# Two loads requested last, products taken two groups sooner and one more tile transposed by DMA, in a fused attention and GLU kernel

## The chip, the core and the metric

The kernel runs on one core of a Trainium2 chip. The metric is the device time of one execution in microseconds. Each run is compared with runs of the kernel before on the same chip in the same rounds. A ratio is the mean time of one kernel's fast runs over the mean of the other's fast runs of the same rounds; it is therefore not quite the ratio of the medians quoted beside it.

## The reference, cut to what matters

x is (1, 2048, 512) in bf16. It is normalized once and feeds two branches.

```python
xn = layernorm(x)
# A: 32 heads of 16, each position attends to 8 positions, 2 apart, at and before it
q, k, v = split(xn @ wqkv)
s = softmax_over_8(q * k_shifted) * v_shifted, summed, @ wo
# B: gated MLP of width 1792
g = silu((gelu(xn @ w_gate) * (xn @ w_up)) @ w_down)
out = x + s * g
```

## The kernel before

The sequence is cut into four chunks of 512 columns, each of four tiles of 128. A chunk goes through glu (14 groups of gate and up), qkv of the next chunk, then down, the attention sums and the output. Tiles 4 to 7 are chunk 1; their transposed form, xnT of chunk 1, is built during chunk 0's glu stage. Work of one stage is hung into the stream of another by `at`, which names the place where it is put into each engine's order.

Names in the lines below: g_ps and u_ps are the gate and up products, ge, u and h what becomes of them, y_ps the down product; pk are the q-k products, L_ps the logits (their sums), E the exponentials, pv the products of E and v, den_ps and o_ps their sums, s_ps the output product; tr is a transpose on TensorE.

```python
    load_x(TPQ, TPQ)
    for i, (lo, hi) in enumerate(((0, DF // 2), (DF // 2, DF))):
        load_w(wg_sb, B_w_gate, lo, hi)
        load_w(wu_sb, B_w_up, lo, hi)
        load_x((2 + i) * TPQ, TPQ)          # x of chunks 2 and 3
    # ...
    def transpose(t, copy=None):            # by TensorE: 4 matmuls, one copy on ScalarE
        tr = mm.tile([P, NC * P], BF16, name="tr", tag="mm")
        to_psum(t, range(NC), tr[:])
        from_psum(t, range(NC), tr[:], copy)
    def transpose_by_dma(t, cs=range(NC)):  # by DMA: one request for each 128x128 block
        for c in cs:
            nc.sync.dma_start(out=xnT[j][:, c, i * P : (i + 1) * P],
                              in_=xns[t][:, c * P : (c + 1) * P], transpose=True)
    # ...
        if i < 2:
            at(("glu", 0, i), transpose, TPQ + i)              # tiles 4 and 5
    # ...
    at(("glu", 0, 9), logits, 0)
    for i in range(8):                      # products of E and v on VectorE
        at(("glu", 0, 11 + i) if i < 3 else ("qkv", 1, 0), av_product, 0, i // 2, i % 2)
    # ...
    at(("glu", 0, 0), transpose_by_dma, TPQ + 2, (0, 1))
    at(("glu", 0, 0), load_v, 0)            # v_arr, four requests, after vT is written
    at(("glu", 0, 0), transpose_by_dma, TPQ + 2, (2, 3))
    at(("glu", 0, 0), transpose_by_dma, TPQ + 3)
    at(("glu", 0, 0), load_late_weights)    # wd, wo
```

All DMA requests above leave from one queue, SyncE's, in program order. The built program gives them eight completion semaphores in turn, so a request also waits until the one eight places before it has landed. v takes a round trip: vst is stored to vT in memory and read back, shifted, as v_arr.

The softmax here doesn't subtract the row's maximum and nothing guards it: scores larger than these inputs give would overflow.

Of the kernel before, what the change touches and what calls it, by code (L numbers as in the profile page):

```python
# [28 lines left out]
def kernel(  # L29
# [15 lines left out]
    DF = B_w_gate.shape[1]  # L45
    NT, NC, NF, NJ = S // P, D // P, DF // P, S // TQ
    TPQ = TQ // P
# [39 lines left out]
    def load_x(t, n=1):  # L87
        nc.sync.dma_start(
            out=x_sb[:, t : t + n, :],
            in_=x2d[t * P : (t + n) * P, :].rearrange("(t p) d -> p t d", p=P),  # L90
        )

    def load_w(dst, src, lo, hi):
        nc.sync.dma_start(
            out=dst[:, :, lo:hi], in_=src.rearrange("(k p) n -> p k n", p=P)[:, :, lo:hi]
        )
# [11 lines left out]
    load_x(3)  # L108
    load_wqkv(3)
    load_x(TPQ, TPQ)  # L110
    for i, (lo, hi) in enumerate(((0, DF // 2), (DF // 2, DF))):
        load_w(wg_sb, B_w_gate, lo, hi)
        load_w(wu_sb, B_w_up, lo, hi)
        load_x((2 + i) * TPQ, TPQ)

    def load_late_weights():
        nc.sync.dma_start(out=wd_sb[:], in_=B_w_down.rearrange("(k p) n -> p k n", p=P))
# [155 lines left out]
    def copy_out(j, fo, ps, i0=0, n=TQ, m=1, copy=None):  # L273

        which, c = divmod(fo, NC)
        if which == 0:
            if "q" not in st[j]:
                st[j]["q"] = qp.tile([P, NC, TQ], BF16, name="q_sb")
            dst = st[j]["q"][:, c : c + m, i0 : i0 + n]
        elif which == 1:  # L280
            dst = k_sb[j][:, c : c + m, PAD + i0 : PAD + i0 + n]
        else:
            if c // 2 not in st[j]["vst"]:
                st[j]["vst"][c // 2] = vsp.tile([P, 2, TQ], BF16, name="vst")
            dst = st[j]["vst"][c // 2][:, c % 2 : c % 2 + m, i0 : i0 + n]
        if copy is None:
            nc.scalar.activation(out=dst, in_=ps, func=AF.Copy)  # L287
        else:
            copy(out=dst, in_=ps)
        if which == 2 and (c + m) % 2 == 0 and i0 + n == TQ:  # L290
            r, lo = slice((c // 2) * 2 * P, (c // 2 + 1) * 2 * P), PAD + j * TQ
            nc.sync.dma_start(
                out=vT[r, lo : lo + TQ].rearrange("(c p) n -> p c n", p=P),
                in_=st[j]["vst"][c // 2][:],
            )

    def qkv(j, fo):
        ps = mm.tile([P, 1, TQ], F32, name="qkv_ps", tag="mm")
        project(ps[:, 0, :], wqkv_sb, fo * P, j)
        copy_out(j, fo, ps[:])  # L300
# [128 lines left out]
    def divide(j):  # L429
        oT = st[j]["oT"] = op.tile([P, NC, TQ], BF16, name="oT")  # L430
        for g in range(0, NC, 2):
            nc.vector.tensor_tensor(  # L432
                out=oT[:, g : g + 2, :],
                in0=st[j]["o"][:, g : g + 2, :],
                in1=st[j]["rb"][:].unsqueeze(1).to_broadcast([P, 2, TQ]),
                op=ALU.mult,
            )

    def glu(j, fc):
        g_ps = mm.tile([P, TQ], F32, name="g_ps", tag="mm")  # L440
        project(g_ps[:], wg_sb, fc * P, j)
        u_ps = mm.tile([P, TQ], F32, name="u_ps", tag="mm")
        project(u_ps[:], wu_sb, fc * P, j)
        ge = sm.tile([P, TQ], BF16, name="ge")
        nc.scalar.activation(out=ge[:], in_=g_ps[:], func=AF.Gelu_apprx_tanh)  # L445
        u = sm.tile([P, TQ], BF16, name="u")
        nc.scalar.activation(out=u[:], in_=u_ps[:], func=AF.Copy)  # L447
        h = hp.tile([P, TQ], BF16, name="h")
        nc.vector.tensor_tensor(out=h[:], in0=ge[:], in1=u[:], op=ALU.mult)  # L449
        st[j][fc] = h  # L450

    def down(j, tt, cols):

        n = cols.stop - cols.start
        y = mm.tile([P, n], F32, name="y_ps", tag="mm")
        for fc in range(NF):
            nc.tensor.matmul(  # L457
                y[:],
                lhsT=st[j][fc][:, tt * P : (tt + 1) * P],
                rhs=wd_sb[:, fc, cols],  # L460
                start=(fc == 0),
                stop=(fc == NF - 1),
            )
        sl = slp.tile([P, n], BF16, name="sl")
        nc.scalar.activation(out=sl[:], in_=y[:], func=AF.Silu)  # L465
        return sl

    def finish(j, tt, cols, sl):

        t, n = j * TPQ + tt, cols.stop - cols.start  # L470
        s = mm.tile([P, n], F32, name="s_ps", tag="mm")
        for g in range(NC):
            nc.tensor.matmul(  # L473
                s[:],
                lhsT=st[j]["oT"][:, g, tt * P : (tt + 1) * P],
                rhs=wo_sb[:, g, cols],
                start=(g == 0),
                stop=(g == NC - 1),
            )
        m = sm2.tile([P, n], BF16, name="m")  # L480
        nc.vector.tensor_tensor(out=m[:], in0=s[:], in1=sl[:], op=ALU.mult)  # L481
        o_t = sm4.tile([P, n], BF16, name="o_t")
        nc.vector.tensor_tensor(out=o_t[:], in0=m[:], in1=x_sb[:, t, cols], op=ALU.add)
        nc.sync.dma_start(out=out2d[t * P : (t + 1) * P, cols], in_=o_t[:])
# [4 lines left out]
    def at(key, fn, *args):  # L489
        side.setdefault(key, []).append((fn, args))  # L490

    def run(stage, j, i):
        for fn, args in side.get((stage, j, i), ()):
            fn(*args)

    for i in range(TPQ):
        at(("down", 0, 1), moments, 2 * TPQ + i)
        if i < 2:
            at(("glu", 0, i), transpose, TPQ + i)
        at(("down", 0, 2), normalize, 2 * TPQ + i)  # L500
        at(("glu", 1, 0) if i else ("down", 0, 3), transpose_by_dma, 2 * TPQ + i)
        at(("glu", 1, 10 + i), moments, 3 * TPQ + i)
        at(("qkv", 2, i), normalize, 3 * TPQ + i)
        at(("glu", 2, 0) if i else ("down", 1, 3), transpose_by_dma, 3 * TPQ + i)
# [2 lines left out]
        at(("glu", 0, w), qk_products, 0, [w], 0, NC)  # L507
    at(("glu", 0, 9), logits, 0)
    for i in range(8):
        at(("glu", 0, 11 + i) if i < 3 else ("qkv", 1, 0), av_product, 0, i // 2, i % 2)  # L510

    def sums(j):

        if j + 1 < NJ:
            nc.scalar.preload_act_table(AF.Exp)
        denominators(j)
        av_sums(j)
        if j + 1 < NJ:
            logits(j + 1)
        reciprocals(j)  # L520
        store_reciprocals(j)
        spread_reciprocals(j)
        if j + 1 < NJ:
            load_v(j + 1)
# [80 lines left out]
    for n, fo in enumerate((0, 2, 4, 6, 8, 10)):  # L605
# [4 lines left out]
            for i in range(2):  # L610
                project(ps[:, i, i0 : i0 + w], wqkv_sb, (fo + i) * P, 0, HQ + i0, w)
        copy_out(0, fo, ps[:], HQ, HQ, 2)
    at(("glu", 0, 0), transpose_by_dma, TPQ + 2, (0, 1))
    at(("glu", 0, 0), load_v, 0)
    at(("glu", 0, 0), transpose_by_dma, TPQ + 2, (2, 3))
    at(("glu", 0, 0), transpose_by_dma, TPQ + 3)
    at(("glu", 0, 0), load_late_weights)
    for j in range(NJ):
        for fc in range(NF):
            run("glu", j, fc)  # L620
            glu(j, fc)
        if j + 1 < NJ:

            for i, fo in enumerate((0, 1, 4, 5, 2, 3, 6, 7, 8, 9, 10, 11)):
                run("qkv", j + 1, i)
                qkv(j + 1, fo)
            full = slice(0, D)
            sl = []
            for tt in range(TPQ):
                run("down", j, tt)  # L630
                sl.append(down(j, tt, full))
                if tt == 0:
                    sums(j)
            divide(j)
            for tt in range(TPQ):
                finish(j, tt, full, sl[tt])
        else:
            full, half = slice(0, D), (slice(0, D // 2), slice(D // 2, D))
            sl = [down(j, tt, full) for tt in range(TPQ - 1)]
            divide(j)  # L640
            finish(j, 0, full, sl[0])
            finish(j, 1, full, sl[1])
            sl3 = down(j, 3, half[0])
            finish(j, 2, full, sl[2])
            finish(j, 3, half[0], sl3)
            sl3 = down(j, 3, half[1])
            finish(j, 3, half[1], sl3)
# [28 lines left out]
```

## Time and profile before

| | before |
|---|---|
| median time of the first three runs | 227.88 us (227.87 to 228.2) |
| span of the profiled run | 226.7 us |
| TensorE, VectorE, ScalarE busy | 98%, 67%, 58% |
| granted TensorE clock | 1.000 |
| transposes of chunk 1 by TensorE, by DMA | tiles 4 and 5, tiles 6 and 7 |

Read the engine shares first: when one engine is busy in 98% of the span, idle time elsewhere costs nothing, and any change must be judged by what it takes from that engine's stream or by the holes that it makes in it. The prediction shows the lines.

### The profile page before, as it was taken

The numbers are of one execution on the slowest core, as the hardware profiler recorded it, in microseconds if no ns is written. First come the engines' busy times: TensorE is split into PE (matmuls) and PEld (weight loads), VectorE is DVE, ScalarE is ACT, GpSimd is POOL, SyncE is SP. The second block draws the span as 40 slices with busy tenths as digits, with TensorE's granted clock in tenths as the row PEclk, the third lists the DMA queues.
The fourth block names the chain that finished last, engine by engine and source line by source line (L and its number), as shares of the span: only waits on it lengthen the run. The fifth ranks groups of instructions, "written<-read, shape, count | busy, mean of one in ns | idle before, by whom it ended". The sixth has DMA issues, their size and how long they took to land.

```text
span 226.7 us, 3637 instructions
## 1 busy us (share of the span) xinstructions
PE 222.4 (98%) x1342; PEld 107.9 (48%) x1342; DVE 152.2 (67%) x281; ACT 132.3 (58%) x209; POOL 21.4 (9%) x67
## 2 busy tenths in 40 slices
PE   8999999999999999999999999999999999999993
PEld 4995444444444444444444444444444444444453
DVE  5588961999995489969803859925934448971434
ACT  4388679767631767676752466676763356756210
POOL 1025961000040000320000000000000000000000
PEclk9999999999999999999999999999999999999999
DMA  6999399942049911100219941100218940001011
GB/s 191 361 397 385 102 211 162 309 121 95 6 99 198 196 48 30 21 1 0 93 34 205 191 112 23 26 6 0 92 25 167 198 113 0 0 3 30 1 39 54
DMA packets 30130, 24.64 MB, mean 109 GB/s; under 512 B 10784, under 2 KB 29600, under 8 KB 30112
## 3 DMA queue, kind: packets, MB, share of 16 engines
q1 hardware_dynamic: 30112, 24.41, 45.1%
q8 instruction: 10, 0.16, 0.3%
q14 instruction: 8, 0.07, 0.1%
HBM read 18.74 MB, written 4.34 MB: 102 GB/s over the span
## 4 chain that ended last, share of the span: by engine, by line
PE 98%; DVE 0%; issue 0%; DVEq 0%
PE y_ps L457 21%; PE g_ps L263 21%; PE u_ps L263 21%; PE qkv_ps L263 16%; PE s_ps L473 6%; PE L_ps L352 3%; PE o_ps L420 3%; PE qk_ps L551 2%; PE v_ps L551 1%; PE warm_ps L245 1%; PE qk_ps L542 1%; PE den_ps L372 0%; PE tr L221 0%; PE v_ps L542 0%; PE trb L221 0%; DVE m L481 0%
## 5 line engine op out<-in xcount | busy, mean ns | idle before, releaser
L263 PE MATMUL g_ps<-xnT,wg_sb 128*128 128x512 bf16 x224 | 57.5, 379 | 0.0
L263 PE MATMUL u_ps<-xnT,wu_sb 128*128 128x512 bf16 x224 | 57.5, 379 | 0.0
L457 PE MATMUL y_ps<-wd_sb,h 128*128 128x512 bf16 (+1 forms) x238 | 49.9, 367 | 0.0
L447 ACT ACTIVATE u<-u_ps 128x512 bf16<-128x512 f32 x56 | 33.5, 598 | 16.9 <-PE u_ps L263 16.9
L445 ACT ACTIVATE ge<-g_ps 128x512 bf16<-128x512 f32 x56 | 33.5, 598 | 16.4 <-PE g_ps L263 16.3
L449 DVE TENSOR_TENSOR h<-ge,u 128x512 bf16<-128x512 bf16 x56 | 23.8, 425 | 28.5 <-ACT u L447 26.9
L334 DVE TENSOR_TENSOR pk<-q_sb,k_sb 128x1024 bf16<-128x1024 bf16 (+1 forms) x56 | 39.0, 760 | 4.6 <-ACT k_sb L287 4.6
L406 DVE TENSOR_TENSOR pv<-E,v_arr 128x1024 bf16<-128x1024 bf16 (+1 forms) x48 | 39.7, 862 | 0.3 <-DMA v_arr<-vT 0.3
L263 PE MATMUL qkv_ps<-xnT,wqkv_sb 128*128 128x512 bf16 (+2 forms) x200 | 37.0, 345 | 0.0
L457 PEld LDWEIGHTS <-h 128*128 128x128 bf16 x238 | 23.0, 98 | 25.9 <-issue 1.3
L263 PEld LDWEIGHTS <-wu_sb 128*128 128x128 bf16 x224 | 21.9, 98 | 26.4
L263 PEld LDWEIGHTS <-wg_sb 128*128 128x128 bf16 x224 | 21.7, 98 | 26.3 <-issue 0.8
L465 ACT ACTIVATE sl<-y_ps 128x512 bf16<-128x512 f32 (+1 forms) x17 | 9.7, 572 | 32.6 <-PE y_ps L457 32.6
L263 PEld LDWEIGHTS <-wqkv_sb 128*128 128x128 bf16 x200 | 18.9, 98 | 17.5
L481 DVE TENSOR_TENSOR m<-s_ps,sl 128x512 bf16<-128x512 f32 (+1 forms) x17 | 11.1, 655 | 18.9 <-PE s_ps L473 18.9
L432 DVE TENSOR_TENSOR oT<-o_ps,rb 128x1024 bf16<-128x1024 f32 x8 | 9.4, 1218 | 11.9 <-DMA rb<-rs_d 11.9
L205 POOL TENSOR_TENSOR rstd<-rstd,mhalf 128x1 f32<-128x1 f32 x12 | 8.1, 671 | 71.5 <-DVE rstd L202 71.5
L473 PE MATMUL s_ps<-wo_sb,oT 128*128 128x512 bf16 (+1 forms) x68 | 14.8, 366 | 0.0
L287 ACT ACTIVATE vst<-qkv_ps 128x512 bf16<-128x512 f32 x14 | 8.4, 597 | 3.7 <-PE qkv_ps L263 3.7
L287 ACT ACTIVATE k_sb<-qkv_ps 128x512 bf16<-128x512 f32 x14 | 8.4, 601 | 3.2 <-PE qkv_ps L263 3.2
L473 PEld LDWEIGHTS <-oT 128*128 128x128 bf16 x68 | 6.7, 98 | 7.2
L287 ACT ACTIVATE q_sb<-qkv_ps 128x512 bf16<-128x512 f32 x14 | 8.3, 603 | 3.0 <-PE qkv_ps L263 3.0
(64 smaller groups left out, 130.7 us busy)
## 6 DMA issues: line engine op xcount, KB each, us to landing
v_arr<-vT SPq DMA_DIRECT2D x16, 520.0 KB, 8.6
vT<-vst SPq DMA_DIRECT2D x8, 256.0 KB, 2.2
out_dram<-o_t SPq DMA_DIRECT2D x15, 128.0 KB, 3.2
wg_sb<-in_B_w_gate_dram SPq DMA_DIRECT2D x2, 896.0 KB, 10.0
wu_sb<-in_B_w_up_dram SPq DMA_DIRECT2D x2, 896.0 KB, 11.6
wd_sb<-in_B_w_down_dram SPq DMA_DIRECT2D x1, 1792.0 KB, 9.4
wqkv_sb<-in_A_wqkv_dram SPq DMA_DIRECT2D x4, 384.0 KB, 4.8
x_sb<-in_A_x_dram SPq DMA_DIRECT2D x3, 512.0 KB, 11.3
```

Source lines behind the costliest of these rows:

```text
L263: nc.tensor.matmul(ps, lhsT=w[:, dk, lo : lo + P], rhs=xnT[j][:, dk, i0 : i0 + n], start=(dk == 0), stop=(dk == NC - 1),)
L287: nc.scalar.activation(out=dst, in_=ps, func=AF.Copy)
L334: nc.vector.tensor_tensor(out=st[j]["pk"][w][:, c0 : c0 + n, :], in0=st[j]["q"][:, c0 : c0 + n, :], in1=k_sb[j][:, c0 : c0 + n, off : off ...
L406: nc.vector.tensor_tensor(out=pv[:, d : d + n, :], in0=st[j]["E"][:, wh, :].unsqueeze(1).to_broadcast([P, n, TQ]), in1=st[j]["va"][:, 4 * ...
L432: nc.vector.tensor_tensor(out=oT[:, g : g + 2, :], in0=st[j]["o"][:, g : g + 2, :], in1=st[j]["rb"][:].unsqueeze(1).to_broadcast([P, 2, TQ ...
L445: nc.scalar.activation(out=ge[:], in_=g_ps[:], func=AF.Gelu_apprx_tanh)
L447: nc.scalar.activation(out=u[:], in_=u_ps[:], func=AF.Copy)
L449: nc.vector.tensor_tensor(out=h[:], in0=ge[:], in1=u[:], op=ALU.mult)
L457: nc.tensor.matmul(y[:], lhsT=st[j][fc][:, tt * P : (tt + 1) * P], rhs=wd_sb[:, fc, cols], start=(fc == 0), stop=(fc == NF - 1),)
L465: nc.scalar.activation(out=sl[:], in_=y[:], func=AF.Silu)
L473: nc.tensor.matmul(s[:], lhsT=st[j]["oT"][:, g, tt * P : (tt + 1) * P], rhs=wo_sb[:, g, cols], start=(g == 0), stop=(g == NC - 1),)
L481: nc.vector.tensor_tensor(out=m[:], in0=s[:], in1=sl[:], op=ALU.mult)
```

## The change

The intent is to take another tile off TensorE. This lengthens the DMA queue, so two other things are moved to make room: loads that nobody needs yet go last, and the products that v_arr feeds go sooner, since v_arr should now be there sooner. Tile 4 stays on TensorE, in the same place.

```diff
-    for i, (lo, hi) in enumerate(((0, DF // 2), (DF // 2, DF))):
+    for lo, hi in ((0, DF // 2), (DF // 2, DF)):
         load_w(wg_sb, B_w_gate, lo, hi)
         load_w(wu_sb, B_w_up, lo, hi)
-        load_x((2 + i) * TPQ, TPQ)
 ...
-        if i < 2:
-            at(("glu", 0, i), transpose, TPQ + i)
 ...
-        at(("glu", 0, 11 + i) if i < 3 else ("qkv", 1, 0), av_product, 0, i // 2, i % 2)
+        at(("glu", 0, 9 + i) if i < 5 else ("qkv", 1, 0), av_product, 0, i // 2, i % 2)
 ...
-    at(("glu", 0, 0), transpose_by_dma, TPQ + 2, (0, 1))
+    at(("glu", 0, 0), transpose, TPQ)
+    at(("glu", 0, 0), transpose_by_dma, TPQ + 1, (0, 1))
     at(("glu", 0, 0), load_v, 0)
-    at(("glu", 0, 0), transpose_by_dma, TPQ + 2, (2, 3))
+    at(("glu", 0, 0), transpose_by_dma, TPQ + 1, (2, 3))
+    at(("glu", 0, 0), transpose_by_dma, TPQ + 2)
     at(("glu", 0, 0), transpose_by_dma, TPQ + 3)
     at(("glu", 0, 0), load_late_weights)
+    for j in (2, 3):
+        at(("glu", 0, 0), load_x, j * TPQ, TPQ)
```

## The prediction

> **What bounds the kernel now.** I read the engine table of the page first, then the chain that ended last, then the order of time on TensorE, on the DMA queue and on VectorE around the places that the change touches.
>
> ```profile
> PE 222.4 (98%) x1342; PEld 107.9 (48%) x1342; DVE 152.2 (67%) x281; ACT 132.3 (58%) x209; POOL 21.4 (9%) x67
> PEclk9999999999999999999999999999999999999999
> PE 98%; DVE 0%; issue 0%; DVEq 0%
> ```
>
> TensorE is busy in 98% of the span and is 98% of the chain; its clock is full in every slice. The time is the sum of what TensorE is given, so only two things can shorten it: fewer or shorter matmuls, or the removal of a gap between them. The chain in order of time shows both kinds of item that this change touches:
>
> ```profile
> 17.34 0.22 PE tr L221 x4
> 17.56 0.86 PE g_ps L263 x4
> 18.43 0.86 PE u_ps L263 x4
> 19.29 0.22 PE tr L221 x4
> ...
> 57.51 1.73 PE o_ps L420 x32
> 59.24 1.80 PE L_ps L352 x32
> ...
> 113.17 1.73 PE L_ps L352 x32
> ```
>
> Columns: start, duration, work. The transposes of tiles 4 and 5 stand in the stream without a gap, 0.22 us for four. The logits of chunk 1 take 1.80 us where those of chunk 2 take 1.73 us for the same 32 matmuls. Looking at single matmuls, one in each of the last two groups of four starts 0.08 us late (60.45 and 60.67 us), just after VectorE's last product of q and k ends:
>
> ```profile
> 45.01 5.76 DVE L406 TENSOR_TENSOR pv<-E,v_arr 128x2048 bf16<-128x2048 bf16 x5
> 50.68 9.71 DVE L334 TENSOR_TENSOR pk<-q_sb,k_sb 128x1024 bf16<-128x1024 bf16 x16
> 60.32 0.95 DVE L385 RECIPROCAL rs<-den_ps 128x128 bf16<-128x128 f32 x1
> ```
>
> So VectorE is about 0.07 us too late there: five products of E and v left over from the glu stage push the sixteen q-k products to 60.39 us. No other wait in the chain exceeds the 0.1 us lost where matmul shapes change. The rest of the profile matters only as a risk. The DMA queue's issues:
>
> ```profile
> 17.12 2.87 SPq L292 DMA_DIRECT2D vT<-vst  x2
> 20.09 2.71 SPq L255 DMA_TRANSPOSE xnT<-xn  x2
> 25.85 2.70 SPq L308 DMA_DIRECT2D v_arr<-vT  x4
> 28.59 8.87 SPq L255 DMA_TRANSPOSE xnT<-xn  x6
> 38.29 0.40 SPq L117 DMA_DIRECT2D wd_sb<-in_B_w_down_dram  x1
> 40.48 2.53 SPq L120 DMA_DIRECT2D wo_sb<-in_A_wo_dram  x4
> ```
>
> **What the Trainium skill says.** (1) "VectorE: DVE Perf Modes", section "The three transpose paths", gives 390 ns for a 128x128 transpose on TensorE and 1309 ns through DMA. This trace: a DMA transpose holds the queue 1.24 us (median), in agreement; but in the full TensorE stream a transpose costs only 0.056 us from start to start. Taking one off TensorE is thus worth 0.056 us, not 0.39. (2) "DMA: Bandwidth & Descriptors", section "Anatomy of one DMA — SWDGE (gpsimd) path", says that DMA engines do not wait on semaphores: waits happen on the issuing sequencer before dispatch. The trace agrees: the queue issues nothing from 22.81 to 25.85 us, and then the first load of v_arr, 0.07 us after the second store of vT has landed (25.78); all transposes behind it wait too. (3) Same page, "Queues, rings and completion order": each engine consumes one queue's descriptors in ring order. The trace agrees: the x of chunk 3, requested at 12.36 us, lands only at 23.77, and the vT stores follow it.
>
> **The change part by part.** *Tile 5 by DMA.* Four TensorE transposes go: 4 x 0.056 = 0.22 us straight off the path. ScalarE loses a copy of 0.59 us and a PSUM buffer is freed; both are off the path. The queue gets four more transposes, 4 x 1.24 = 5 us of issue, and xnT of chunk 1 must be complete when TensorE starts that chunk's qkv, now at 43.74 us and 0.22 earlier after.
>
> *x of chunks 2 and 3 last.* They are 2 x 512 KB = 1.05 MB ahead of the vT stores. The engines move 396 to 405 GB/s in 10 to 20 us, so the vT stores land about 2.6 us sooner: 25.8 - 2.6 = 23.1 us (tile 5's first two transposes have left the queue at 22.8, so they don't hold it). The loads of v_arr start there. They move at some 190 GB/s, and landed one after the other at 31.5, 34.2, 38.3 and 40.5 us; less 2.7: 28.8, 31.5, 35.6 and 37.8.
>
> *When is tile 7 done?* After the v loads come ten transposes. The issue waits on eight completion semaphores used in turn: a request waits until the one eight places before has landed. The trace shows it twice: wd leaves at 38.29, when the third v load has landed (38.28), and the first wo at 40.48, when the fourth has (40.47). In the changed order the four v loads are followed by two blocks of tile 5, four of tile 6 and four of tile 7 (a block is one 128x128 transpose); eight places after the third v load comes tile 7's first block, after the fourth its second. By issue time alone the first would be ready to leave at 33 to 34 us, so it waits for the load at 35.6, and the second for the load at 37.8. So: second block issued at 37.8, third at 39.1, fourth at 40.3, each landing some 2.3 us after its issue on an idle DMA (as the later, unqueued transposes do), the last at about 42.6 us. TensorE needs blocks in order, the first at 43.5 and the fourth three matmuls (0.65 us) later, 44.2. The margin is about 1.6 us. The wd load leaves at 41.6 instead of 38.3; its 1.8 MB at 388 GB/s land at about 48.3, and TensorE needs them at 54. The x of chunk 2 lands before 53 and is first used by VectorE at 59 or later.
>
> *Products of E and v two groups sooner.* Their v_arr is there at 37.8 instead of 40.5, so five instead of three fit into the glu stage. A period is 1.73 us and holds one h (0.34 from start to start) and one product (1.14): it fits. The first of them can hold the next h until about 39.0, where h came at 38.85 before: no buffer of three is short of it. Two products, 2 x 1.15 = 2.3 us, leave the stretch behind the stage, less some 0.4 because the last glu products queue behind each other; the q-k products end near 58.5 instead of 60.4, which removes the 0.07 us at the logits. Everything else that VectorE gains is off the path.
>
> Sum: -0.22 - 0.07 = -0.29 us: 227.88 - 0.29 = 227.6 us, 0.13%.
>
> **The rivals.** *A DMA turns late.* If the v loads come sooner by only 1 us or less, tile 7's second block leaves after 39.5 us and its fourth lands after 44.3: TensorE waits in front of chunk 1's qkv. With no shift at all (40.5) the last block lands at 45.3, 1.1 us late, and the first held h makes it a little more: 229 us. For it: the margin rests on the FIFO order, and one transpose in the trace took 2.36 us instead of 1.24. Against: the 1.05 MB lie fully ahead of the stores and the engines are saturated from 5 to 23 us, and the odd transpose would fall before the wait for the third load. *VectorE in order holds the glu stage.* The first E-v product now stands in front of the h of group 9; if v_arr lands at 40 us or later, ScalarE runs out of ge buffers at group 12 (about 41 us) and TensorE out of PSUM: up to 1 to 2 us more, 228.5 to 229.5. Against: the landing at 37.8. *A large gain* (the earlier E, reciprocals and loads of chunk 1 pull the rest): nothing speaks for it, as no TensorE gap waits for these; it would stay at 227.6. *Nothing:* the 0.29 us is below the spread of the three runs (227.87 to 228.2), so the median may well read unchanged.
>
> **Range and chances.** If the margin holds, the result is 227.6 with some 0.2 of scatter; one in ten for a stall of 0.5 to 1.5 us. Range 227.25 to 228.2. 2% is 4.6 us: the gain cannot reach it, since nothing but 0.3 us leaves TensorE, and a loss of it would need all stalls at once.
>
> **What would show it.** In the changed profile: 1338 matmuls instead of 1342; one group of four tr in front of the glu stage instead of two; g_ps of group 1 directly behind u_ps; L_ps of chunk 1 at 1.73 us; v_arr issued at about 23.1 us; the last transposes issued at 38 to 41.5 us; the chain still TensorE at 98%, with no wait in front of the first qkv_ps of chunk 1 (about 43.7 us on the chain). Wrong would be: a gap of TensorE at 43.5 us released by DMA, or gaps between g_ps and u_ps in 38 to 43 us.

## The result, and the profile after

The changed kernel took 227.6 us in the median of six runs (227.47 to 228.57), the kernel before 228.09 us (227.87 to 228.25) in six runs of the same rounds. The ratio is 0.9988 with a 95% interval of 0.997 to 1.0006: by these times alone no gain is clear of the noise. The forecast was 227.6 us, inside a range of 227.25 to 228.2.

The profiled execution was, by chance, the slowest of the six, at 228.57 us. This makes the page look as if nothing was won:

```profile
span 226.8 us, 3616 instructions
...
PE 220.7 (97%) x1317; PEld 106.9 (47%) x1338; DVE 151.9 (67%) x281; ACT 131.9 (58%) x208; POOL 28.0 (12%) x67
...
PE 86%; DVE 6%; DMA 3%; ACT 1%; issue 1%; SPq 1%; ACTq 0%; DVEq 0%
```

Two readings here need care. The matmul count of 1317 is not 1338 because some matmul records are missing from a trace; the weight loads, one for each matmul, are complete at 1338, four fewer than before. The chain now runs partly over VectorE and ScalarE. That is no sign of a new wait: where a matmul's record is missing, the chain can step to another engine. One y_ps record is missing just before 57.55 us, for instance, and there the chain goes back to pk. The order of time of the chain shows what happened to TensorE (start, duration, work). Of the kernel before:

```profile
12.07 5.27 PE qkv_ps L263 x56
```

Of the changed kernel:

```profile
3.14 5.93 DMA x_sb<-in_A_x_dram
...
12.62 5.27 PE qkv_ps L262 x56
17.89 0.22 PE tr L220 x4
...
57.84 1.73 PE o_ps L419 x32
59.57 1.73 PE L_ps L351 x32
...
113.43 1.73 PE L_ps L351 x32
```

The first full qkv group starts 0.55 us later, because the load of x of tile 2 landed late in this execution (5.93 us under way, first line). Then there is one group of transposes instead of two. The sums of chunk 0 (o_ps) are 0.33 us behind those of the kernel before instead of 0.55: 0.22 us have been won. The logits of chunk 1 take 1.73 us instead of 1.80.

To be free of the start, I read the starts of single matmuls from each trace and cut the time between the first full qkv_ps matmul and the last s_ps matmul into stretches. They repeat to 0.01 us from one execution to the next where nothing waits, so this ruler settles differences that the total time, with its scatter of some 0.6 us, cannot. All numbers are us; the rest of the kernel, from the first y_ps after the logits of chunk 1 to the last s_ps, is 161.95 us in every kernel in this table, to within 0.01.

| kernel | first full qkv_ps starts | to first g_ps | to logits of chunk 0 | to chunk 1's qkv | to first y_ps | to the y_ps after logits of chunk 1 | sum with rest |
|---|---|---|---|---|---|---|---|
| before | 11.91 | 5.49 | 15.86 | 10.49 | 10.36 | 6.87 | 211.02 |
| after | 12.46 | 5.49 | 15.63 | 10.49 | 10.36 | 6.80 | 210.72 |
| e1, tile 5 only | 11.84 | 5.50 | 15.63 | 10.49 | 10.45 | 6.80 | 210.82 |
| e2, x last only | 11.94 | 5.49 | 15.86 | 10.49 | 10.36 | 6.84 | 210.99 |
| e3, E-v products only | 11.81 | 5.49 | 15.86 | 10.49 | 10.36 | 7.58 | 211.73 |
| e4, x last and tile 5 | 11.91 | 5.49 | 15.63 | 10.49 | 10.36 | 6.84 | 210.77 |
| e5, after again | 11.94 | 5.49 | 15.63 | 10.49 | 10.36 | 6.80 | 210.72 |
| e7, tiles 4 to 7 on TensorE | 11.48 | 5.49 | 16.30 | 10.49 | 10.36 | 7.52 | 212.12 |
| e8, e1 with wo early | 11.88 | 5.49 | 15.63 | 11.72 | 13.51 | 6.80 | 215.11 |
| e9, tile 4 by DMA too | 11.60 | 5.27 | 15.63 | 10.49 | 10.45 | 6.80 | 210.59 |
| e10, tile 5 ahead of v | 11.68 | 5.49 | 15.63 | 10.49 | 10.36 | 7.29 | 211.22 |
| e11, most of tile 4 by DMA | 12.01 | 5.33 | 15.63 | 10.49 | 10.79 | 6.80 | 210.99 |

Between before and after, 0.23 us are gone from the stretch that held tile 5's transposes, 0.07 us from the one with the logits, and nothing else has changed: 0.30 us in all. The medians differ by 0.49 us in these rounds and by 0.36 us in those of e5; the start (11.48 to 12.46 us in the table) and the landing of v_arr vary from run to run by enough to make such differences, but nothing here shows that they did.

The DMA queue of the changed kernel (start, duration of the issue, request, count):

```profile
17.68 1.23 SPq L291 DMA_DIRECT2D vT<-vst  x2
19.01 3.06 SPq L254 DMA_TRANSPOSE xnT<-xn  x2
24.14 2.83 SPq L307 DMA_DIRECT2D v_arr<-vT  x4
27.02 15.50 SPq L254 DMA_TRANSPOSE xnT<-xn  x10
42.56 0.58 SPq L116 DMA_DIRECT2D wd_sb<-in_B_w_down_dram  x1
```

The loads of v_arr leave 1.7 us sooner than before, though the start was 0.55 us later. The ten transposes need 15.5 us instead of ten times 1.24, because there is a wait inside. The view of what the SyncE queue waited for (us in total, times, longest) says what ended it:

```profile
SPq L254 <- DMA v_arr<-vT: 1.9, 2, 1.6
```

Single requests and landings from the trace: seven of them have gone by 37.0 us; the next, tile 7's second block, leaves at 38.64, and the fourth load of v_arr has landed at 38.62. In the trace this request waits for the semaphore on which that load lands. The last block lands at 43.63, while its matmul comes at 44.72.

VectorE, in order of time:

```profile
46.10 3.49 DVE L405 TENSOR_TENSOR pv<-E,v_arr 128x2048 bf16<-128x2048 bf16 x3
49.51 9.72 DVE L333 TENSOR_TENSOR pk<-q_sb,k_sb 128x1024 bf16<-128x1024 bf16 x16
59.14 0.95 DVE L384 RECIPROCAL rs<-den_ps 128x128 bf16<-128x128 f32 x1
```

Three products of E and v are left over instead of five. The sixteen q-k products end at 59.23 instead of 60.39 us, before the logits matmuls that need them.

### The profile page after: what moved, and what is told of

The parts are those of the page before. It is cut to its first block, busy times and chain, and to the rows that moved or that the text cites. A ratio compares the mean times of both kernels' runs of the same rounds, so it can differ in the third digit from the quotient of the medians.

```text
span 226.8 us, 3616 instructions
## 1 busy us (share of the span) xinstructions
PE 220.7 (97%) x1317; PEld 106.9 (47%) x1338; DVE 151.9 (67%) x281; ACT 131.9 (58%) x208; POOL 28.0 (12%) x67
## 4 chain that ended last, share of the span: by engine, by line
PE 86%; DVE 6%; DMA 3%; ACT 1%; issue 1%; SPq 1%; ACTq 0%; DVEq 0%
PE u_ps L262 21%; PE y_ps L456 20%; PE g_ps L262 20%; PE qkv_ps L262 12%; PE s_ps L472 6%; DVE pk L333 3%; PE L_ps L351 3%; PE o_ps L419 3%; DMA x_sb<-in_A_x_dram 3%; ACT u L446 1%; DVE pv L405 1%; SPq L100 1%; DVE stats L187 1%; PE den_ps L371 0%; PE tr L220 0%
## 5 line engine op out<-in xcount | busy, mean ns | idle before, releaser
L262 PE MATMUL g_ps<-xnT,wg_sb 128*128 128x512 bf16 x218 | 56.5, 379 | 0.2
L456 PE MATMUL y_ps<-wd_sb,h 128*128 128x512 bf16 (+1 forms) x233 | 49.3, 366 | 0.2
L456 PEld LDWEIGHTS <-h 128*128 128x128 bf16 x238 | 23.1, 98 | 25.9 <-issue 1.3
```

The source lines that it names most:

```text
L262: nc.tensor.matmul(ps, lhsT=w[:, dk, lo : lo + P], rhs=xnT[j][:, dk, i0 : i0 + n], start=(dk == 0), stop=(dk == NC - 1),)
L456: nc.tensor.matmul(y[:], lhsT=st[j][fc][:, tt * P : (tt + 1) * P], rhs=wd_sb[:, fc, cols], start=(fc == 0), stop=(fc == NF - 1),)
```

## The experiments

My theory: the gain is the four transposes and the short wait at the logits; x last is what makes room for the longer queue, because tile 7's blocks hang on the landing of v_arr through the reused semaphores; the sooner products are only safe with v_arr sooner. Rivals: the gain or part of it comes from the move of x itself; the transposes wait for nothing but their place in the queue; a tile on TensorE costs more than its matmuls.

Each kernel was correct.

### e1: tile 5 by DMA alone

The second and the last part of the change (without load_x), on the kernel before:

```diff
-        if i < 2:
-            at(("glu", 0, i), transpose, TPQ + i)
-    at(("glu", 0, 0), transpose_by_dma, TPQ + 2, (0, 1))
+    at(("glu", 0, 0), transpose, TPQ)
+    at(("glu", 0, 0), transpose_by_dma, TPQ + 1, (0, 1))
     at(("glu", 0, 0), load_v, 0)
-    at(("glu", 0, 0), transpose_by_dma, TPQ + 2, (2, 3))
+    at(("glu", 0, 0), transpose_by_dma, TPQ + 1, (2, 3))
+    at(("glu", 0, 0), transpose_by_dma, TPQ + 2)
```

> Only tile 5 goes to DMA; x of chunks 2 and 3 stays ahead of the vT stores, E-v products stay at groups 11 to 13. Theory (transposes wait for the completion semaphore eight places back): v_arr lands as before at about 40.5 us, tile 7's second block leaves only then, its fourth lands at about 45.3, and TensorE stands about 1.1 us in front of chunk 1's qkv; net of the 0.22 us saved +0.9 us, ratio about 1.004. Rival A (only ring order and issue time count, 10 blocks of 1.3 us from 28.6): last block lands at about 44, no wait, -0.22 us, ratio 0.999. Rival B: the transposes delay v_arr too, and the loss exceeds 2 us.

Measured: 228.63 us median (227.85 to 228.88), ratio 1.0014 (1.0001 to 1.0027). Two of six runs were at 227.85 and 228.0, four at 228.58 to 228.88. The profile is of the 228.0 us run. In it v_arr had landed early, at 39.29 where the theory had 40.5, tile 7's second block left at 39.31 and the fourth landed at 44.15, just when its matmul was due (44.11); TensorE lost 0.09 us there. The request left 0.02 us after the landing, as the theory says. That the four slower runs waited longer at this place is likely, but no profile of one of them shows it. Even so, tile 5 alone doesn't pay: its interval lies above 1, that of the same edit with x last (e4) below 1.

### e2: x of chunks 2 and 3 last, alone

```diff
-        load_x((2 + i) * TPQ, TPQ)
+    for j in (2, 3):
+        at(("glu", 0, 0), load_x, j * TPQ, TPQ)
```

> Only x of chunks 2 and 3 is requested last. Theory: v_arr's loads leave at about 23 to 24 us and land at 38 to 38.6 instead of 40.5, and no TensorE item changes: time as before, ratio 1.000 within 0.001. Rival: the move itself gives time (less traffic in the first 25 us lets TensorE start sooner): the first full qkv_ps group starts before 12.0 us in the profile and the ratio is 0.998 or less.

Measured: 228.39 us (227.82 to 228.48), ratio 1.0001 (0.9989 to 1.0013). The v_arr loads left at 23.34 and had landed at 37.59, 2.9 us sooner than before. The sum of stretches is 210.99 against 211.02, and the start was 11.94 against 11.91. The move by itself gives nothing; the rival falls.

### e3: E-v products two groups sooner, alone

```diff
-        at(("glu", 0, 11 + i) if i < 3 else ("qkv", 1, 0), av_product, 0, i // 2, i % 2)
+        at(("glu", 0, 9 + i) if i < 5 else ("qkv", 1, 0), av_product, 0, i // 2, i % 2)
```

> Only the products of E and v come two groups sooner, with v_arr still landing at about 40.5 us. Theory: VectorE stands in front of h of group 9 until 40.5, h follows at 41.7, ScalarE lacks a ge buffer at group 12 and TensorE a PSUM buffer: up to 1 us lost at 40 to 44 us, less 0.07 us at the logits of chunk 1; ratio 1.002 to 1.004. Rival: the three ge and u buffers and four PSUM buffers take up the whole delay: no TensorE gap, ratio 0.9995 to 1.0005.

Measured: 228.29 us (228.0 to 228.99), ratio 1.0007 (0.9995 to 1.002). VectorE did stand from 34.4 to 40.5 us, and ScalarE did lack a ge buffer at group 12:

```profile
40.45 0.60 ACT L447 ACTIVATE u<-u_ps 128x512 bf16<-128x512 f32 x1 [0.27 <-PE u_ps L263]
42.18 0.60 ACT L445 ACTIVATE ge<-g_ps 128x512 bf16<-128x512 f32 x1 [1.13 <-DVE h L449]
```

The bracket says that ScalarE was idle for 1.13 us until an h freed a buffer. But the stretches up to 10.36 are unchanged: the four PSUM buffers took up this wait, as the rival said. The loss, 0.71 us in the profile (7.58 against 6.87), came later and from another cause, as the chain shows:

```profile
51.37 9.65 DVE pk L334 x16
61.02 0.04 issue
61.06 0.59 PE L_ps L352 x5
```

The products held back in the stage pile up behind it, so the q-k products end at 61.02 instead of 60.39 and the last logits matmuls wait. The profile is of the slowest of the six runs, and the ratio of all six is not clear of 1, so this loss is shown for that execution alone. Neither the theory nor the rival had this place right.

### e4: x last and tile 5 by DMA, products where they were

The edits of e1 and e2 together.

> The change without its E-v part. Theory: 0.22 us of TensorE transposes go, the logits of chunk 1 keep 1.80 us; from the first full qkv_ps group to the last matmul 0.22 us less than before, ratio 0.999. Rival: the sooner E-v products carry most of the gain, and this run reads as before (1.000), or the later transposes make TensorE wait at chunk 1's qkv (1.001 or more).

Measured: 228.0 us (227.58 to 228.28), ratio 0.9987 (0.9975 to 0.9999). The sum is 210.77, 0.25 us less than before. The logits stretch is 6.84, between 6.87 and 6.80: the sooner products are worth only the last 0.04 or 0.05 us. The last block of tile 7 landed at 43.05, in time.

### e5: the changed kernel again

No edit.

> The changed kernel once more, for a narrower interval and a second profile. Theory: from the first full qkv_ps group to the last s_ps matmul 210.72 us as in the first profile (before 211.02), whatever the start; the first full qkv_ps group starts anywhere in 11.8 to 12.5 us as the first loads land; ratio 0.9985 to 0.9990. Rival: the change itself makes the start later (12.46 us in the first profile against 11.91 of before): again 12.3 or later, and the ratio nearer to 1.000.

Measured: 227.85 us (227.78 to 228.04), ratio 0.9986 (0.9972 to 1.0). The sum is 210.72 to the hundredth, and the start 11.94: the late start of the first profile was that execution's, not the change's. Its chain has, for the line at 12.62 above:

```profile
12.10 5.28 PE qkv_ps L262 x56
```

### e7: tiles 6 and 7 on TensorE too

On the kernel before, with two tiles added to TensorE where the change takes one away:

```diff
-        if i < 2:
-            at(("glu", 0, i), transpose, TPQ + i)
+        at(("glu", 0, i), transpose, TPQ + i)
-    at(("glu", 0, 0), transpose_by_dma, TPQ + 2, (0, 1))
-    at(("glu", 0, 0), transpose_by_dma, TPQ + 2, (2, 3))
-    at(("glu", 0, 0), transpose_by_dma, TPQ + 3)
```

> The kernel before with tiles 6 and 7 transposed on TensorE as well, none of chunk 1 by DMA: the cost of a tile on TensorE, doubled. Theory: two tiles at 0.22 us each, 211.46 us from the first full qkv_ps group to the last matmul (before 211.02), less 0.07 at most elsewhere; ratio about 1.002. Rival: a tile on TensorE costs more than its matmuls (the ScalarE copy of 0.59 us and a PSUM buffer hold up the glu stage): 0.6 us or more for the two tiles.

Measured: 228.81 us (228.56 to 229.06), ratio 1.0027 (1.0015 to 1.004). The stretch before the logits grew from 15.86 to 16.30, 0.44 us for two tiles: the price of 0.22 us a tile holds, and the copies on ScalarE cost nothing in this stretch. The rest of the loss, 0.65 us at the logits of chunk 1, I had not expected. In this execution v_arr landed at 41.13 us, 0.66 us after that of the kernel before, although no transpose stood behind it, and the q-k products ended at 61.07. Taking the transposes away had a side effect: wd was requested at 28.56 instead of 38.29, right behind the loads of v_arr, and these took 15.33 us from the first issue to the last landing, where the other fast profiles have 14.04 to 14.65. That wd slowed them is likely and was not tested. So the kernel before lives with an edge: its logits wait as soon as v_arr is late. (The first wo request took 10.09 us to issue in this run, and no landing ended it: a request can be held in other ways too. Nothing waited for it.)

### e8: e1 with the suspected wait enlarged

wo's four loads (0.5 MB) are also requested before the vT stores, on top of e1.

```diff
+    for j in range(WL):
+        nc.sync.dma_start(out=wo_sb[H * j : H * (j + 1), :, :], in_=...)
     def load_late_weights():
         nc.sync.dma_start(out=wd_sb[:], ...)
-        for j in range(WL):
-            nc.sync.dma_start(out=wo_sb[H * j : H * (j + 1), :, :], in_=...)
```

> Tile 5 by DMA alone (as e1) with wo's four loads, 0.5 MB, also ahead of the vT stores: the suspected wait enlarged. Theory (tile 7's second block leaves when the fourth v_arr load lands, its fourth block lands 4.85 us after that, as in e1: 39.30 and 44.15): v_arr lands at 40.6 to 42, tile 7's last block at 45.5 to 47, and the stretch from the first qkv_ps of chunk 1 to its first y_ps grows from 10.36 us to 11.7 to 13, one for one with the landing; time 1.2 to 2.5 us over the kernel before. Rival: transposes are not held by the landing (they are in the ring already) and the last block lands within 1 us of v_arr's end: stretch below 10.6 us, time as e1.

Measured: 232.33 us in the median of the three fast runs (231.08 to 232.61), ratio 1.0167 (1.0138 to 1.0197). A fourth run, at 234.66, counts as slow. v_arr had landed at 42.02, tile 7's second block left at 42.03, and its four blocks landed at 44.68, 44.88, 45.54 and 46.78. TensorE in order of time (the bracket is the idle time before the group and what ended it):

```profile
44.72 0.60 PE L263 MATMUL qkv_ps<-xnT,wqkv_sb 128*128 128x512 bf16 x2 [1.07 <-DMA xnT<-xn]
45.58 0.39 PE L263 MATMUL qkv_ps<-xnT,wqkv_sb 128*128 128x512 bf16 x1 [0.25 <-DMA xnT<-xn]
46.83 3.33 PE L263 MATMUL qkv_ps<-xnT,wqkv_sb 128*128 128x512 bf16 x8 [0.86 <-DMA xnT<-xn]
50.38 8.02 PE L263 MATMUL qkv_ps<-xnT,wqkv_sb 128*128 128x512 bf16 x36 [0.22 <-issue]
```

The first, the third and the fourth matmul start 0.04 to 0.05 us after their blocks have landed. This shows the wait, its place and its cause. The loss is larger than I expected: the brackets come to 1.07 + 0.25 + 0.86 = 2.18 us, but the two stretches grew by 1.23 + 3.15 = 4.38 us. Part of this is the measure: a bracket counts from the modelled end of the matmul before. From start to start, less the usual 0.216, these three matmuls are late by 1.24 + 0.41 + 1.03 = 2.68 us. 1.70 us are left. The third line says why: eight matmuls take 3.33 us. The same place by stretches of time (window and length, busy time of PE, PEld, DVE, ACT and POOL, granted clock, DMA share, GB/s):

```profile
43.60:46.80 3.20, 1.04 (x4) 0.21 (x3) 3.20 (x6) 0.60 (x1) 0.00 (x0) 1.00 0.10 21
46.80:48.80 2.00, 1.97 (x6) 0.78 (x7) 2.00 (x2) 0.60 (x1) 0.00 (x0) 0.58 0.74 218
48.80:50.40 1.60, 1.38 (x5) 0.48 (x5) 1.60 (x3) 0.60 (x1) 0.00 (x0) 0.50 1.07 378
50.40:52.40 2.00, 2.00 (x9) 0.91 (x9) 2.00 (x3) 1.20 (x3) 0.00 (x0) 0.96 1.06 377
```

From 47.14 us the clock stood at half for 3.41 us, and matmuls started 0.427 us apart instead of 0.216. Half of 3.41 is 1.70 us, so the two together make up the 4.38. The runs fit this: the mean clock was 1.000 in the run of 231.08 us, 0.993 in those of 232.33 and 232.61, and 0.985 in that of 234.66. The Trainium skill, "TensorE: Matmul & The Clock Gate", section "What's actually happening", describes this: a window of 3413 ns in which TensorE is idle sends the clock to half. The length agrees. But no idle window of that length was needed here: the longest single wait was 1.07 us, and in the 3.41 us before the clock fell TensorE was idle for 2.1 us.

### e6 and e9: tile 4 by DMA as well

To beat both kernels, the four blocks of tile 4 were put on the queue ahead of the vT stores, where it stands idle.

```diff
     sum_constants()
+    transpose_by_dma(TPQ)
 ...
-    at(("glu", 0, 0), transpose, TPQ)
```

> The changed kernel with tile 4 by DMA too, its four blocks issued ahead of the vT stores, where the queue stands idle from 12.9 to 17.7 us. Theory: 0.22 us more off TensorE, 210.50 us from the first full qkv_ps group to the last matmul, ratio about 0.9977; v_arr's loads leave by 24.5 us and chunk 1's qkv waits for nothing. Rival: the four blocks hold the vT stores until 21 us, v_arr comes 1 us or more later than in the changed kernel (38.6), the last block of tile 7 after 44.5, and TensorE waits 0.3 to 1 us at chunk 1's qkv: ratio 0.999 to 1.002.

Measured: the profile (294.52 us, clock 0.757) is not used. The four fast runs gave 228.2 to 228.39 us, ratio 1.0005 (0.9991 to 1.0019): no gain. So the same kernel was run again for a profile.

> e6 again, as its profile fell in a slow state (clock 0.757): where did its 0.22 us go? Theory: TensorE has four transposes fewer before the glu stage (10.27 us less 5.05 from tile 4, so 0.22 us less up to the logits), but the vT stores leave after 21 us, v_arr lands at 39.3 us or later, tile 7's last block 4.85 us after it, and the stretch from the first qkv_ps of chunk 1 to its first y_ps is 0.3 to 1 us over 10.36. Rival: no wait there, and the loss is in the start (first full qkv_ps group at 12.3 us or later).

(The figures in the first bracket of that text are muddled; what is meant is 5.49 less 0.22 in the stretch to the first g_ps.) Measured: 227.64 and 227.77 us, two runs, ratio 0.9979 (0.9961 to 0.9997). The stretch is 5.27, 0.22 less, as expected. v_arr landed at 38.55 and tile 7's last block at 43.69, 0.05 us after its matmul was due, and 0.09 us are lost there, less than the 0.3 to 1 us expected, as v_arr came sooner than 39.3. The sum, 210.59, is the smallest of all kernels here. Why the runs of e6 were some 0.6 us slower than these two is not settled: the margin at chunk 1's qkv is gone in this version, so a v_arr that lands later would cost time one for one, but no profile of a fast run of e6 exists.

### e10: all of tile 5 ahead of the v_arr loads

```diff
-    at(("glu", 0, 0), transpose_by_dma, TPQ + 1, (0, 1))
+    at(("glu", 0, 0), transpose_by_dma, TPQ + 1)
     at(("glu", 0, 0), load_v, 0)
-    at(("glu", 0, 0), transpose_by_dma, TPQ + 1, (2, 3))
```

> The changed kernel with all four blocks of tile 5 ahead of the v_arr loads, so that only eight transposes follow them and only the last needs the fourth load's landing. Theory: v_arr leaves at 23.5 to 24.5 as before, tile 7's last block lands about 2.4 us after the fourth load (40.5 to 41.5) instead of 5.0 us after it; 210.72 us from the first full qkv_ps group to the last matmul, ratio 0.9986 as the changed kernel; the margin at chunk 1's qkv grows from about 1 us to 2.5 us or more. Rival: issue time and not the landing sets the last block: it lands at 42.5 us or later as in the changed kernel (43.2).

Measured: 227.94 us (227.8 to 228.24), ratio 0.9991 (0.9979 to 1.0004). v_arr landed at 39.77, the last transpose left at 39.78 and landed at 42.62, 2.85 us after v_arr instead of 5.0: with eight transposes behind the loads, only the last one hangs on the fourth landing, as the theory says. (The rival had named 42.5 us or later, and the block did land later, but it left 0.02 us after the landing of v_arr.) But the loads themselves left at 25.11, because one of the blocks ahead of them took 2.93 us to issue, and the logits of chunk 1 paid for it: 7.29 instead of 6.80. In this execution, the slowest of the five, what was gained as margin at one place was lost at the other.

### e11: e10 with three of tile 4's blocks by DMA

One block ahead of the vT stores, two behind v_arr, the last on TensorE (transpose_block is a helper for one block).

```diff
+    transpose_by_dma(TPQ, (0,))             # after sum_constants()
-    at(("glu", 0, 0), transpose, TPQ)
+    at(("glu", 0, 0), transpose_block, TPQ, 3)
+    at(("glu", 0, 0), transpose_by_dma, TPQ, (1, 2))   # after load_v
```

> e10 with three of tile 4's four blocks by DMA: one ahead of the vT stores, two behind the v_arr loads. Theory: three blocks of 0.056 us leave TensorE, 210.55 us from the first full qkv_ps group to the last matmul; tile 7's last block lands some 4.9 us after the fourth v_arr load, at 43 to 43.5 us, just in time; ratio 0.998. Rival: the one block ahead of the stores delays v_arr by 0.5 us or more, and TensorE waits at chunk 1's qkv: ratio 0.9995 or more.

Measured: 227.65 us (227.57 to 228.39), ratio 0.9976 (0.9962 to 0.999). The profile is of the slowest of the five. In it three blocks are gone from the first stretch (5.33 against 5.49), but v_arr landed at 39.55, the last block at 44.50, and TensorE waited:

```profile
44.54 1.67 PE L267 MATMUL qkv_ps<-xnT,wqkv_sb 128*128 128x512 bf16 x7 [0.27 <-DMA xnT<-xn]
```

That cost 0.43 us. The other four runs, at 227.57 to 227.71, were 0.68 to 0.82 us faster; no profile shows whether they were without the wait. This version has the lowest ratio of all, and e9's two runs come near it, but e9 is the kernel of e6, whose four fast runs showed no gain. The intervals overlap with those of the changed kernel, so neither is shown to beat it.

## Why the prediction was right, point by point

What was forecast and found is the mechanism: 0.29 us expected, 0.30 us gone from the two stretches named, and no wait in the others. That the median reads 227.6 to the digit is luck: the forecast started from 227.88, the median of three runs, and the kernel before read 228.09 in six.

- **Four transposes at 0.056 us.** Right: the stretch lost 0.23 us in the changed kernel, e1 and e4, and two more tiles cost 0.44 in e7.
- **0.07 us at the logits.** Right in the profile: 6.87 to 6.80. But it was read from one execution in which v_arr landed at 40.47. In e7 the same wait was 0.65 us longer. The gain is thus 0.07 us or more, depending on when v_arr lands.
- **x last moves the v_arr loads to 23.1 us.** Nearly: 24.14 and 23.82 in the two profiles of the changed kernel, 23.34 in e2. The last store of vT landed at 24.05 and 23.73, not at 23.1. The sum was 0.1 off (25.8 - 2.6 is 23.2). The shift itself held for the request ahead of the stores, the small one of zeros (24.16 before, 21.62 after); but the second store then landed 1.66 us after the first instead of 0.86, and why is not shown.
- **Tile 7's blocks hang on the third and fourth v_arr load.** Right, and this was the step that mattered. The second block left 0.02 us after the fourth landing in the changed kernel twice, in e1, e4 and e8.
- **Margin of 1.6 us.** Right in kind, too large: the last block landed at 43.63 with its matmul at 44.72 (1.1 us), and 43.20 against 44.20 in e5 (1.0 us). The mis-sized terms are the landing of v_arr, 38.62 and 38.20 instead of 37.8, and the time from there to the last block's landing, 5.0 us instead of 4.8. The first profile's matmul was due 0.5 us later too. wd, too, landed at 50.5 instead of 48.3, and x of chunk 2 at 53.9 instead of before 53; nothing waited for either.
- **Five products fit into the glu stage.** Right: the q-k products ended at 59.23 (58.80 in e5) against a forecast of about 58.5.
- **The rival of a late queue.** Real, as e1, e8 and e11 show, but it didn't happen in the changed kernel's profiles. I put its price at the wait alone; in e8 2.68 us of waiting cost 4.38, as the clock fell to half after it.
- **The rival of VectorE holding the glu stage.** Its mechanism is only half right: ScalarE ran out of ge buffers (1.13 us in e3), but TensorE did not stall in the stage. The loss fell at the logits of chunk 1, through the q-k products (61.02 us).
- **What would show it.** I wrote that the chain would still be TensorE at 98%. The page says 86%, through missing matmul records and the late first loads, with no new wait in the stretches where nothing was predicted to wait.
- **1309 ns and 1.24 us in agreement.** Read with care: 1.24 us is the time to issue a DMA transpose; to its landing the profile has 2.4 us in the median. The page does not say which of the two its figure is.

## What to carry to other kernels

When one engine is busy all the time, a change is worth what it takes out of that engine's stream, at the start-to-start price there, and the work is to show that nothing that was moved comes late. Follow each moved transfer through its queue, and include the reuse of completion semaphores: a request can be held by the landing of one eight places before it. Compare stretches between fixed instructions rather than total times when the gain is smaller than the scatter of the first loads.

## What the Trainium skill lacked or had wrong

- "VectorE: DVE Perf Modes", "The three transpose paths", gives 390 ns for a 128x128 transpose on TensorE; "TensorE: Matmul & The Clock Gate", "Part 4: PE-mode transpose", gives 390 ns alone and about 275 ns in a kernel. Both are durations of one; neither says what one costs in a full stream. Here one lasts 0.22 us in the trace and costs 0.056 us from start to start: 0.23 us less for four removed, 0.44 us more for eight added.
- "TensorE: Matmul & The Clock Gate" gives an idle window of some 3.4 us as what halves the clock; elsewhere it says, without a figure, that frequent short idles can do so too. In e8 2.18 us of idle time in three pieces, the longest 1.07 us, within 3.2 us was enough; the half clock then lasted 3.41 us.
- No page says that a DMA request can be held by a completion semaphore that an earlier request still owns. In the changed kernel a transpose left 0.02 us after the fourth v_arr load landed, 1.6 us after its predecessor's issue had ended.
